# Three changes of order in a four-layer attention and MLP kernel: VectorE's products of blocks 2 and 3, PSUM banks named by hand, and GpSimd's masks behind a normalisation

## The chip, the cores and the metric

One core of a Trainium2 chip runs the whole kernel. Its engines are TensorE (PE in the profile; PEld is its weight load), VectorE (DVE), ScalarE (ACT), GpSimd (POOL) and SyncE (SP, which here only issues DMAs). The metric is device time in microseconds of one execution. The kernel before was run three times: 746.05, 749.81 and 750.95 us, median 749.81 us.

## The reference

Input `x` has 2048 tokens (S) of 576 features (D), in bfloat16. Four residual layers follow one another: A, B, A, B, the two A's with the same weights and the two B's too.

```python
def _A_ref(x, wqkv, wo):          # 32 heads of 18 features
    q, k, v = ...                  # x @ wqkv, split in heads
    phi = lambda t: jnp.where(t > 0, t + 1, jnp.exp(t)) + 1e-6
    pq, pk = phi(q), phi(k)
    kv = einsum("bhsd,bhse->bhde", pk, v);  z = einsum("bhsd->bhd", pk)
    num = einsum("bhqd,bhde->bhqe", pq, kv)
    den = einsum("bhqd,bhd->bhq", pq, z)[..., None] + 1e-6
    return heads_joined(num / den) @ wo
def _B_ref(x, w1, b1, w2, b2):     # F = 4608
    h = gelu(layernorm(x) @ w1 + b1)
    return h @ w2 + b2
x = x + _A_ref(layernorm(x));  x = x + _B_ref(layernorm(x));  # and both again
```

A is linear attention: the keys of all 2048 tokens have to be summed before any output exists, and each output is divided by a denominator of its own head and token.

## The kernel before

**Layout.** The tokens are cut into 16 tiles of 128 (index `t`) and into 4 blocks of 512 (index `c`, four tiles each). `x_sb` holds all of x; `yT` holds the normalised x with the features on the partitions, which is what the projections read; `units` is a set of 37 slots of 128x512 that hold the queries `pq[(g, c)]` of five groups of heads (`g`) and later the MLP's hidden values.

**Order.** All engines' instructions are recorded in the program's order: the wrapper classes (L53) and `pe` (L229) chain each engine's instructions as they are written. What an engine does next is thus fixed by the source, and a wait of one instruction holds all that stand behind it on that engine.

**PSUM.** The eight banks have names. `accA` and `accB` are pairs of banks and are given out in turn by `pair()`; `one0` to `one3` are single banks, given out in turn by `one()`, which counts `one_turn["n"]` up and takes it modulo 3 or 4. A tag that is given by hand leaves the counter alone. A matmul that opens a bank waits until its last reader is done.

**Layer A, first part (the first layer only: `placed` is False).** A loop over the 16 tiles. In iteration `t` TensorE transposes the normalised tile `t+2` (`tp`, L468), computes the keys of tile `t+1` (`k_ps`, two halves), and adds tile `t` into `rk_ps` and `side_ps`; in five of the iterations (1, 2, 3, 8 and 14) it also projects a query tile (`q_ps`). VectorE in the same iteration (`mid_tile0`, `k_finish`) normalises tile `t+3` (`y_ring`), takes the statistics of tile `t+4` (`ln_st`, `ln_mv`), and then finishes the keys of tile `t+1` (a `phi_e`, and two `pk` instructions, the last of which frees a key bank). GpSimd turns the variance into 1/sqrt (`ln_u`, `ln_rstd`), which the next iteration's normalisation waits for. Ten batches of masks (`mask_batches`: memsets and `affine_select`s for `maskz`, `zsel`, `head_sel`, `quad_mask`, and `head_bc` in four batches called `spread`) are made by GpSimd in iterations 2 to 11, one in each, released by the `pk` that ends `k_finish`.

**Layer A, second part (both A layers).** The sums become a matrix `kvwo` of each group of heads, and the queries that are left are projected. `wo_stage` computes the output of block 0's four tiles, and VectorE adds each to `x_sb` (`residual`); the four tiles are normalised for the MLP at once (the list `first`: two by ScalarE, two by VectorE) and transposed through `tp` banks, while TensorE goes on with `q_next` (a query tile each) and ends with `q_batch`, which does the last four query tiles together in four banks. ScalarE reads each query bank twice (Exp, Relu); in `q_batch` ScalarE and VectorE read one each.

**Layer A, third part.** The denominators of blocks 1 to 3 are computed (`den_stage`), inverted (`reciprocal`), written to DRAM and read back spread over the heads (`spread`, into `yT`). `scales(c)` multiplies block `c`'s five query tiles with them: five VectorE instructions (four of 128x512, one of 128x256), `units<-yT,units`, each of which waits for its own DMAs. `outputs(c)` is two `wo_pair`s: 36 matmuls each on row tiles into one pair of banks and two single ones, and then three VectorE additions into `x_sb`, which free the banks. `groups(n)` puts groups of the next MLP's first product between (`m1_group`: four hidden blocks in a pair, `hp_ps`, and two singles, `h_ps`, evicted by ScalarE with gelu). The third part's order is in the last lines of `layer_A`. TensorE's part of it: two groups, the denominators, four groups, outputs 1, a group, outputs 2, a group, outputs 3.

**Layer B.** For each block the rest of its nine groups, and then `m2_ps` = hidden values times w2, added to `x_sb`.

Of the kernel before, what the change touches and what calls it, by code (L numbers as in the profile page):

```python
# [35 lines left out]
def build(tc, A_x, A_wqkv, A_wo, B_w1, B_b1, B_w2, B_b2, out, n_layers=4):  # L36
    nc = tc.nc
    with ExitStack() as ctx:
# [22 lines left out]
        SYNC = mybir.DependencyInfo(mybir.DependencyClass.Sync, mybir.DependencyReason.DATA)  # L61
        vec, act = InOrder(nc.vector, "VectorE"), InOrder(nc.scalar, "ScalarE")
# [16 lines left out]
        one_turn = dict(n=0, banks=4)  # L79
# [122 lines left out]
        units = const.tile([P, NF + 1, CB], BF16, name="units")  # L202
# [28 lines left out]
        def row_tiles(ops_of, dst, relay, after):  # L231


            order = [(hi, op) for step in zip([op for n in (0, 1, 2, 3) for op in ops_of(n, 0)],
                                              [op for n in (2, 3, 0, 1) for op in ops_of(n, 1)]) for hi, op in enumerate(step)]
            first, final, total = {}, {}, [0] * 4
            for i, (hi, (n, _, _)) in enumerate(order):
                first.setdefault((hi, n), i)
                final[(hi, n)] = i
                total[n] += 1  # L240
            relay_at = {max(final[(0, a)], final[(1, b)]): (a, b) for a, b in ((0, 2), (1, 3))}
            starts = {first[(1, 0)]: 0, first[(0, 2)]: 2, first[(1, 1)]: 1, first[(0, 3)]: 3}
            relay_of, seen = {}, [0] * 4
            for i, (hi, (n, wt, mv)) in enumerate(order):
                ins = mm(dst[n], wt, mv, seen[n] == 0, seen[n] == total[n] - 1)
                seen[n] += 1
                if i in starts:
                    tc.add_manual_dep(ins.ins, relay_of[starts[i]], SYNC, reason="row tiles take turns on a PSUM bank")
                if i in relay_at:
                    passed = relay()  # L250
                    tc.add_manual_dep(passed.ins, ins.ins.name, SYNC, reason="row tiles take turns on a PSUM bank")
                    for m in relay_at[i]:
                        relay_of[m] = passed.ins.name
                after(n, [a == b for a, b in zip(seen, total)], relay_at.get(i))
# [247 lines left out]
        def by_token(ap, placed):  # L502

            return ap.rearrange("p (t b q) -> p b t q", t=4, b=4) if placed else ap

        def as_read(ap, placed):
            return ap.rearrange("p (b t q) -> p b t q", b=4, t=4) if placed else ap
# [21 lines left out]
        def warm_table(func):  # L529
            act.activation(out=act_dummy[:, 0:1], in_=neg_half[:, 0:1], func=func)  # L530
# [21 lines left out]
        def layer_A(li, next_kind, begin, before_tile, before_keys, mid_tile, rows_ahead, after_tile, q_tiles, placed, mlp):  # L552
# [21 lines left out]
            def k_sum(t, half):  # L574
                cols = slice(half * HALF, (half + 1) * HALF)
                vec.tensor_scalar(out=es[t][:, cols], in0=es[t][:, cols], scalar1=1.0, scalar2=1e-6, op0=ALU.min, op1=ALU.add)
                return vec.scalar_tensor_tensor(out=pks[t][:, cols], in0=kps.pop((t, half))[:, 0:HALF], scalar=0.0,
                                                in1=es[t][:, cols], op0=ALU.max, op1=ALU.add)
# [82 lines left out]
            def q_batch(es, tags):  # L661
                c = q_left[0][1]
                del q_left[0:4]
                dst = [(one_of if tag in ("accA", "accB") else one)("q_ps", tag) for tag in tags]

                def ops_of(g, hi):
                    rows, cols = HALVES[hi], slice(c * CA, (c + 1) * CA)
                    ops = [(g, wq_sb[rows, k, g, :], yT[rows, k, cols]) for k in range(KD - 1)]
                    if g % 2 == hi:
                        ops.append((g, q_tail[:, g // 2, :] if hi else wq_sb[rows, KD - 1, g, :], yT[rows, KD - 1, cols]))  # L670
                    return ops

                evicted = set()

                def after(n, done, turn):
                    if not done[n] or n in evicted:
                        return
                    evicted.add(n)
                    to = pq[(n, c)] = units[:, slot_of[(n, c)], :]
                    e = es[n]  # L680
                    act.activation(out=by_token(e, placed), in_=as_read(dst[n][:], placed), func=ACT.Exp)
                    vec.tensor_scalar(out=by_token(to, placed), in0=as_read(dst[n][:], placed), scalar1=0.0, scalar2=None, op0=ALU.max)
                    q_late.append(lambda: q_sum(to, e))

                row_tiles(ops_of, [q[:] for q in dst], relay_by_pool, after)
# [122 lines left out]
            def q_sum(dst, e):  # L808
                vec.tensor_scalar(out=e, in0=e, scalar1=1.0, scalar2=1e-6, op0=ALU.min, op1=ALU.add)
                vec.tensor_tensor(out=dst, in0=dst, in1=e, op=ALU.add)  # L810
# [10 lines left out]
            def finish(n):  # L821
                for _ in range(n):
                    q_late.pop(0)()

            def q_next(late=False, tag=None, between=None, evict=None):
                q_proj(*q_left.pop(0), late, tag, between, evict)
# [21 lines left out]
            for t in range(0 if placed else NT):  # L848
# [15 lines left out]
                if t == 1:  # L864
                    done = k_sum(2, 1)
                mid_tile(t)
                rows_ahead(t)
                if 1 < t < NT - 1:
                    done = k_finish(t + 1)
# [175 lines left out]
            first = [Norm(t, "B", "act" if i < 2 else "dve", "act" if i < 2 else "dve") for i, t in enumerate((0, 2, 1, 3))]  # L1045
# [50 lines left out]
            for t in range(TPC):  # L1096
                wo_stage((0, 2, 1, 3)[t])
                if t == 1:
                    first[0].norm()
                first[t].stats()  # L1100
                first[t].rstd()
                if t == 2:
                    first[1].norm()
                if t == (0 if placed else 1):
                    q_next(True)
                if t == 3:
                    first[0].transposed()
            other = [("accA", "accB")[(pair_turn["n"] + i) % 2] for i in (1, 0)]
            q_next(True)
            first[2].norm()  # L1110
            q_next(True, other[0])
            first[1].transposed()
            q_next(True, other[1])
            if placed:
                q_next(True)
            first[3].norm()
            finish(1)
            first[2].transposed()
            first[3].transposed((other[0],))
            finish(3)  # L1120
            q_batch([units[:, i, :] for i in range(13, 17)], ("one2", "one1", "one3", other[1]))
            warm_table(ACT.Gelu_apprx_tanh)
            assert not q_left

# [1 line left out]
            def scales(c):  # L1126
                for g in range(G):
                    scale_stage(g, c)

            def groups(n, late=()):  # L1130

                for i in range(n):
                    last = bool(late) and i == n - 1
                    mlp.m1_group(0, mlp.done, relay_by_pool, elsewhere)
                    if last:
                        for step in late:
                            step()
                    mlp.flush()

            def outputs(c):  # L1140
                for j in range(2):
                    wo_pair(c, j)
# [10 lines left out]
            spread(3)  # L1153
            scales(1)
            groups(4)
            scales(2)
            outputs(1)
            groups(1)
            scales(3)
            outputs(2)  # L1160
            groups(1)
            outputs(3)

# [115 lines left out]
        norms = [Norm(t, "A", "act" if t == 3 else "dve", "halves" if t < 3 else "act", t < 3) for t in range(NT)]  # L1279
# [54 lines left out]
        batches = mask_batches()  # L1334
# [4 lines left out]
        def before_keys0(t, ys):  # L1339
            if 0 < t < NT - 2:  # L1340
                norms[t + 2].transposed()
                ys[t + 2] = norms[t + 2].y

        def mid_tile0(t):
            if t == 0:
                return
            ahead = [norms[t + 4].stats, norms[t + 4].rstd] if t + 4 < NT else []
            if t + 3 < NT:

                ahead.insert(2 if t == 2 else 0, norms[t + 3].norm)  # L1350
            for step in ahead:
                step()

# [3 lines left out]
        def after_tile0(t, done):  # L1357
            for _ in range(2 if t == 1 else 1):
                if late_pieces:
                    late_pieces.pop(0)()  # L1360
            if 2 <= t < 2 + len(batches):
                first = batches[t - 2]()
                tc.add_manual_dep(first.ins, done.ins.name, SYNC, reason="beside VectorE's statistics")
            if t == NT - 1:
                transpose_b1()

# [61 lines left out]
```

## Time and profile before

| | |
|---|---|
| median of three runs | 749.81 us |
| the profiled execution's own time | 747.97 us |
| its span in the profile | 746.2 us |
| granted TensorE clock, mean | 0.999 |
| VectorE busy | 272.0 us (36%) |
| ScalarE busy | 297.3 us (40%) |
| GpSimd busy | 132.2 us (18%) |
| first A layer, tiles' loop | about 11 to 55 us |
| first A layer, block 0's outputs to the last query | about 66 to 81 us |
| first A layer, blocks 1 to 3 | about 89 to 129 us |
| second A layer, blocks 1 to 3 | about 454 to 493 us |

The span runs from the first to the last instruction of the program; the execution's own time has some 1.8 us more around it. The stages' times are read from the timeline by the names of the tiles. In the timeline a row merges like instructions: start, duration of the whole row, engine, line, operation, tiles, shapes, count, and in brackets how long the engine was idle before it and what ended that idle time. The chain of work that ended last is given as start, length and what ran.

### The profile page before, as it was taken

What the parts mean: (1) busy time and instruction counts of PE and PEld (TensorE: products, weight loads), DVE (VectorE), ACT (ScalarE), POOL (GpSimd) and SP (SyncE); (2) the same over time, 40 slices, a digit from 0 to 9 for tenths busy, and PEclk for the clock granted to TensorE, in tenths of its full rate; (3) what the DMA queues carried; (4) which work ended last, traced back from release to release, by engine and by line L of the source; (5) the groups of instructions that cost most, each with busy time, mean ns of one, the idle gap of its engine ahead of it and who ended that gap; (6) DMA issues with size and microseconds to landing.
All of it is one profiled execution on the core that took longest, in us unless ns stands there. A gap on an engine that the chain in (4) does not pass through costs nothing.

```text
span 746.2 us, 16672 instructions
## 1 busy us (share of the span) xinstructions
PE 738.9 (99%) x6951; PEld 475.9 (64%) x6951; DVE 272.0 (36%) x674; ACT 297.3 (40%) x642; POOL 132.2 (18%) x403
## 2 busy tenths in 40 slices
PE   8999999999999999999999999999999999999998
PEld 4666556774477457646777665777646754774476
DVE  8878725533124402400366685542401140100000
ACT  5766652106700750274035666320273047106700
POOL 4641000322122201200213120021200120010010
PEclk9999999999999999999999999999999999999999
DMA  7946120022011202110023101202000200020000
GB/s 201 241 152 209 64 85 19 8 53 44 2 22 39 44 2 32 44 30 2 17 72 92 33 1 36 69 1 52 18 1 9 52 10 1 16 45 10 1 9 25
DMA packets 61297, 34.74 MB, mean 47 GB/s; under 512 B 37126, under 2 KB 61222, under 8 KB 61222
## 3 DMA queue, kind: packets, MB, share of 16 engines
q1 hardware_dynamic: 60470, 33.45, 17.8%
q8 instruction: 54, 0.88, 0.5%
q10 hardware_dynamic: 752, 0.23, 0.1%
q14 instruction: 21, 0.17, 0.1%
HBM read 21.70 MB, written 4.93 MB: 36 GB/s over the span
## 4 chain that ended last, share of the span: by engine, by line
PE 94%; DVE 3%; ACT 1%; DMA 1%; POOL 1%; issue 0%; SPq 0%; DVEq 0%; POOLq 0%
PE m_ps L229 38%; PE hp_ps L229 20%; PE h_ps L229 17%; PE k_ps L229 4%; PE q_ps L229 4%; PE wo_ps L229 4%; PE rk_ps L229 3%; DVE ln_st L53 1%; DVE y_ring L53 1%; PE side_ps L229 1%; ACT units L53 0%; PE tp L468 0%; DVE units L53 0%; DMA yT<-rden_rows 0%; POOL ln_rstd L53 0%
## 5 line engine op out<-in xcount | busy, mean ns | idle before, releaser
L229 PEld LDWEIGHTS <-units 128*128 128x128 bf16 (+1 forms) x2926 | 266.1, 97 | 67.9 <-issue 3.6
L229 PE MATMUL m_ps<-w_sb,units 128*128 128x288 bf16 (+2 forms) x2288 | 283.0, 286 | 0.0
L229 PEld LDWEIGHTS <-w_sb 64*128 64x128 bf16 x2304 | 127.7, 94 | 133.6 <-issue 4.0
L229 PE MATMUL h_ps<-yT,w_sb 64*128 64x512 bf16 x1152 | 174.0, 376 | 0.0
L229 PE MATMUL hp_ps<-yT,w_sb 64*128 64x512 bf16 x1152 | 151.4, 376 | 1.7 <-DVE x_sb L53 1.7
L53 DVE TENSOR_TENSOR x_sb<-m_ps,xo 128x576 bf16<-128x576 f32 (+3 forms) x34 | 24.4, 721 | 323.7 <-PE m_ps L229 323.7
L53 ACT ACTIVATE units<-hp_ps,b1T 128x512 bf16<-128x512 f32 x144 | 91.2, 684 | 88.5 <-PE hp_ps L229 88.5
L53 ACT COPY relay_sb<-relay_sb 128x1 f32<-128x1 f32 x112 | 21.4, 191 | 235.6 <-PE hp_ps L229 224.7
L53 ACT ACTIVATE units<-h_ps,b1T 128x512 bf16<-128x512 f32 x142 | 95.2, 687 | 0.0
L53 POOL TENSOR_TENSOR xo<-x_sb,b_bc 128x576 f32<-128x576 bf16 x32 | 40.8, 1274 | 302.8 <-DVE x_sb L53 291.3
L229 PE MATMUL k_ps<-wkv_sb,yT 64*128 64x288 bf16 (+3 forms) x432 | 61.4, 299 | 0.4 <-ACT yT L53 0.2
L229 PE MATMUL hp_ps<-yT,w_tail 64*128 64x512 bf16 x144 | 54.1, 376 | 0.0
L229 PE MATMUL h_ps<-yT,w_tail 64*128 64x512 bf16 x144 | 54.1, 376 | 0.0
L53 DVE BATCH_NORM_STATS2 ln_st<-x_sb 128x6 f32<-128x288 bf16 x128 | 51.2, 440 | 1.1 <-DMA x_sb<-in_A_x_dram 0.8
L53 DVE STREAM_TRANSPOSE shared<-y_ring 128x640 bf16<-128x640 bf16 x40 | 32.9, 826 | 41.2 <-DMA yT<-shared 39.1
L53 ACT ACTIVATE phi_e<-k_ps 128x288 bf16<-128x288 f32 x64 | 26.3, 413 | 54.0 <-PE k_ps L229 50.2
L53 DVE TENSOR_SCALAR y_ring<-x_sb,ln_mv,ln_rstd 128x576 bf16<-128x576 bf16 (+2 forms) x60 | 33.3, 557 | 24.5 <-POOL ln_rstd L53 24.0
L229 PEld LDWEIGHTS <-yT 64*128 64x128 bf16 (+1 forms) x448 | 36.4, 95 | 8.9 <-ACT yT L53 0.5
L229 PE MATMUL q_ps<-yT,wq_sb 64*128 64x512 bf16 (+2 forms) x282 | 41.9, 349 | 0.0
L53 POOL MEMSET pool_relay<- 128x1 f32 x152 | 16.7, 110 | 127.9 <-PE hp_ps L229 45.4
L229 PE MATMUL wo_ps<-shared,units 64*128 64x288 bf16 (+1 forms) x480 | 38.0, 283 | 0.0
L229 PEld LDWEIGHTS <-w_tail 64*128 64x128 bf16 x288 | 27.1, 94 | 16.9
(110 smaller groups left out, 501.4 us busy)
## 6 DMA issues: line engine op xcount, KB each, us to landing
yT<-shared SPq DMA_DIRECT2D x160, 40.0 KB
w_sb<-in_B_w_dram SPq DMA_DIRECT2D x12, 432.0 KB
w_sb<-in_B_w_dram SPq DMA_DIRECT2D x9, 512.0 KB
yT<-rden_rows SPq DMA_DIRECT2D x24, 126.0 KB
y_rows<-y_ring SPq DMA_DIRECT2D x16, 144.0 KB
units<-y_rows SPq DMA_DIRECT2D x16, 144.0 KB
x_sb<-in_A_x_dram SPq DMA_DIRECT2D x15, 144.0 KB
out_dram<-x_sb SPq DMA_DIRECT2D x15, 144.0 KB
```

What stands on the lines that cost most here:

```text
L53: inst = issue(*args, **kw)
L229: return pe(nc.tensor.matmul(out_, lhsT=lhsT, rhs=rhs, start=start, stop=stop, **kw))
```

## The change

Three parts, all of them a matter of order or place. No instruction is added or taken out on any engine, and TensorE's, ScalarE's, GpSimd's and SyncE's orders are as before; VectorE's order changes in the third part of both A layers alone.

1. **Products behind outputs.** The third part's order, seen by VectorE, was products 1, products 2, additions 1, products 3, additions 2, additions 3. It becomes products 1, additions 1, products 2, additions 2, products 3, additions 3.
2. **Banks by hand.** In the first A layer's second part the query tiles and transposes take banks that are named, and `one_turn["n"]` is set to 3 behind `q_batch`. In the order of TensorE, the banks of the twelve opened there were one1, one2, one3, accA, one0, accB, one1, accA for query, transpose, query, query, transpose, query, transpose, transpose, and one2, one1, one3, accB for the batch's four; they become one0, one2, accA, one1, one3, one0, one2, accA, and accB, one3, one1, one2. From there to the end of the next MLP the single banks are the same turn shifted by two.
3. **Masks behind a normalisation.** Batch `i` was issued at the end of iteration `i+2` behind the last `pk` of `k_finish`; it is issued in iteration `i+3` behind that iteration's normalisation. On GpSimd it stands in the same place between two tiles' `ln_rstd`.

```diff
@@ second part
                 if t == (0 if placed else 1):
-                    q_next(True)
+                    q_next(True, None if placed else "one0")
                 if t == 3:
-                    first[0].transposed()
+                    first[0].transposed((None if placed else "one2",))
             other = [("accA", "accB")[(pair_turn["n"] + i) % 2] for i in (1, 0)]
-            q_next(True)
+            q_next(True, None if placed else other[0])
             first[2].norm()
-            q_next(True, other[0])
-            first[1].transposed()
-            q_next(True, other[1])
+            q_next(True, other[0] if placed else "one1")
+            first[1].transposed((None if placed else "one3",))
+            q_next(True, other[1] if placed else "one0")
             if placed:
                 q_next(True)
             first[3].norm()
             finish(1)
-            first[2].transposed()
+            first[2].transposed((None if placed else "one2",))
             first[3].transposed((other[0],))
             finish(3)
-            q_batch([units[:, i, :] for i in range(13, 17)], ("one2", "one1", "one3", other[1]))
+            q_batch([units[:, i, :] for i in range(13, 17)],
+                    ("one2", "one1", "one3", other[1]) if placed else (other[1], "one3", "one1", "one2"))
+            if not placed:
+                one_turn["n"] = 3
@@ third part
             scales(1)
             groups(4)
+            outputs(1)
             scales(2)
-            outputs(1)
             groups(1)
+            outputs(2)
             scales(3)
-            outputs(2)
             groups(1)
             outputs(3)
@@ masks
+        def norm_and_masks(t):
+            norms[t + 3].norm()
+            if 2 < t < 3 + len(batches):
+                first = batches[t - 3]()
+                tc.add_manual_dep(first.ins, vec.last, SYNC, reason="beside VectorE's statistics")
+
         def mid_tile0(t):
...
-                ahead.insert(2 if t == 2 else 0, norms[t + 3].norm)
+                ahead.insert(2 if t == 2 else 0, lambda: norm_and_masks(t))
...
-            if 2 <= t < 2 + len(batches):
-                first = batches[t - 2]()
-                tc.add_manual_dep(first.ins, done.ins.name, SYNC, reason="beside VectorE's statistics")
```

## The prediction

> **What bounds the kernel now.** I read the page's busy shares first, then its chain that ended last, and then the chain and the timeline of the three stretches that the change touches.
>
> ```profile
> PE 738.9 (99%) x6951; PEld 475.9 (64%) x6951; DVE 272.0 (36%) x674; ACT 297.3 (40%) x642; POOL 132.2 (18%) x403
> ...
> PE 94%; DVE 3%; ACT 1%; DMA 1%; POOL 1%; issue 0%; SPq 0%; DVEq 0%; POOLq 0%
> ```
>
> TensorE is the bound: 94% of the chain is its own work, which the change does not touch. The change can only win stretches in which TensorE stood still, so I took the distance from each matmul's start to the next one's and looked where it is longer than the columns need. Behind the start (up to 12 us) only these are over 0.2 us: 0.25 at 43.3 and 0.25 at 46.2 (masks), 0.41 at 76.0 (banks), 0.21 at 81.7, 1.85 at 110.2 (products) and 0.20 at 388.8. All that the change could remove is thus some 3 us of 746.
>
> **Part 1, products behind outputs.** The timeline of the first A layer:
>
> ```profile
> 105.67 0.90 PE L229 MATMUL wo_ps<-shared,units 64*128 64x288 bf16 x10
> ...
> 107.70 1.43 DVE L53 TENSOR_TENSOR units<-yT,units 128x512 bf16<-128x512 bf16 x4 [4.88 <-DMA yT<-rden_rows]
> ...
> 111.14 0.29 DVE L53 TENSOR_TENSOR units<-yT,units 128x256 bf16<-128x256 bf16 x1 [2.00 <-DMA yT<-rden_rows]
> 111.34 2.87 DVE L53 TENSOR_TENSOR x_sb<-wo_ps,x_sb 128x576 bf16<-128x576 f32 x6
> 112.14 1.04 PE L229 MATMUL hp_ps<-yT,w_sb 64*128 64x512 bf16 x8 [1.69 <-DVE x_sb L53]
> ```
>
> Outputs 1 start at 105.67. Their six additions stand on VectorE behind block 2's products, whose fifth waits until 111.14 for a DMA. The next group (`hp_ps`) needs the bank of the first addition and starts at 112.14, 6.47 us after the outputs did. In the second A layer that DMA was earlier, and the same stretch has no stall:
>
> ```profile
> 471.16 0.90 PE L229 MATMUL wo_ps<-shared,units 64*128 64x288 bf16 x10
> ...
> 475.80 1.04 PE L229 MATMUL hp_ps<-yT,w_sb 64*128 64x512 bf16 x8
> ...
> 479.68 0.77 PE L229 MATMUL wo_ps<-shared,units 64*128 64x288 bf16 x9
> ```
>
> There it is 475.80 - 471.16 = 4.64 us. So the first layer loses 6.47 - 4.64 = 1.83 us, the second nothing.
>
> With the new order the additions wait for the outputs' matmuls alone, as those of outputs 2 do already: in the first layer these start at 116.03, their additions at 118.45 and 120.66, 2.42 and 4.63 us later, three in 1.49 us, and the next group starts at 120.44 without a stall. So the 1.83 us go. What is late next? Block 2's products now start behind the last addition. From a start W of outputs 1: the last three additions at W + 4.86 (4.63, and 0.23 more, as this stretch takes 4.64 where that of outputs 2 takes 4.41), done at W + 6.35; five products, 1.34 to the fifth's start and 0.29 for it, done at about W + 8.0; outputs 2 start at W + 4.64 + 3.88 (475.80 to 479.68) = W + 8.52. Half a microsecond is left. For block 3: additions done at 4.63 + 1.49 = 6.12, products at 7.8, outputs 3 at 4.41 + 3.88 = 8.29: again 0.5. The DMAs are no limit there: block 2's last data came 5.5 us after W (111.14 - 105.67), block 3's were used at 116.41, 10.7 after W, where the new order asks for them at about W + 14. Five waits move onto TensorE's weight loads of the first five operands; all are over by then, so I count them as nothing. **Value: -1.83 us in the first layer, 0 in the second.** Ends: -2.0, and, if the margin of 0.5 fails by as much in all four places, +2.0 - 1.83 = +0.2.
>
> **Part 2, banks.** Rows around the last transposes:
>
> ```profile
> 74.37 2.06 ACT L53 ACTIVATE units<-q_ps 128x512 bf16<-128x512 f32 x4
> ...
> 75.95 0.18 DVE L53 COPY y_ring<-y_ring 128x64 bf16<-128x64 bf16 x1
> ...
> 76.48 0.44 PE L468 MATMUL tp<-ident,y_ring 128*128 128x128 bf16 x5 [0.25 <-ACT units L53]
> ```
>
> ScalarE reads two query tiles here, the first until 75.46 and the second until 76.43. The last transpose takes `accA`, before the change the second's bank; its data are ready at 75.95 + 0.18 = 76.13. After it, `accA` is the first's bank, free at 75.46, so the transposes start at about 76.17, 0.31 earlier. The batch behind them then opens `one1`, the second's bank, with its second matmul, which can start at 76.43 + 0.05 = 76.48 instead of 76.87: 0.39 gained over the two. Inside the batch one start lies 0.12 us late at 78.06, where `accB` waits for the next query tile, read until 78.00; after the change the batch's fourth bank is `one2`, last copied out by VectorE at 77.26, just before it is wanted (76.46 + 4 steps of 0.24 = 77.4). The stall of 0.21 us at 81.74 stays: the hidden block that starts there takes, before and after, the bank of the batch's third tile, evicted at 82.11 by VectorE behind ScalarE, and that work follows TensorE forward. ScalarE itself runs without a gap from 70.7 to 78.0, from the first normalisation's 1/sqrt on, so it does not follow these 0.4 us; the banks it frees are those I used. The closest new wait is the query tile that now takes `accA`: free at 71.66 (third block-0 addition), wanted at 72.04. **Value: -0.5 us.** Ends: -0.7 (the third stall too) and +0.3 (that margin used up and nothing gained).
>
> **Part 3, masks.** The chain in the tiles' loop:
>
> ```profile
> 40.18 0.58 POOL ln_rstd L53
> 40.76 0.03 issue
> 40.78 0.94 DVE y_ring L53
> 41.73 0.73 DVE ln_st L53 x2
> ...
> 43.09 0.58 POOL ln_rstd L53
> 43.66 0.03 issue
> 43.69 0.94 DVE y_ring L53
> ```
>
> A normalisation starts when the 1/sqrt ends, and so does the mask batch; the two collide. Alone it takes 0.42 us (14.41), beside the `head_bc` batch 0.94, beside `quad_mask`'s select and `head_bc`'s memset 1.35 (34.14). The tile then takes 2.91 us (40.78 to 43.69) on this chain, where TensorE needs 2.66 (transposes at 25.45, 28.11 and 30.77). From the transposes at 30.77 to those at 48.46 there are six tiles and one query tile: 17.69 us, against 6 x 2.66 + 1.08 = 17.04. **0.65 us are lost in all.**
>
> After the change the batch starts when the normalisation ends. Its neighbours are then the statistics, which take 0.44 and 0.44 us beside a 0.64 us select (32.05) and without one (36.0) alike. But GpSimd's next 1/sqrt stands behind the batch: 0.42 + 0.06 (a wait's delay, 18.56 to 18.62) + 1.40 (batch at 40.75) + 0.3 + 0.6 (`ln_u`, `ln_rstd`) = 2.78 us a tile, still 0.12 over TensorE's 2.66, for the three `spread` batches that a 1/sqrt follows: 0.36, less what the earlier batches, now shorter, leave in hand. I take 0.2 us of stall left: **-0.45 us.** Ends: -0.65, and +0.5, if `phi_e` is held as the normalisation was.
>
> That is where a rule speaks against the change. The rows: beside a select the statistics keep their 0.44 us and the normalisation loses 0.5. The Trainium skill (SBUF — State Buffer, Who interferes with whom) says that VectorE in a two-port mode and GpSimd share a port pair, held for a whole instruction by whichever issued first, and that an instruction with one SBUF input outside these modes doesn't contend; the rows fit. By that rule the batch's tail now blocks the `phi_e`.
>
> **The sum:** -1.83 - 0.5 - 0.45 = -2.8 us. Nothing behind gives it back: from the last query to 129 us TensorE had no other stall over 0.1 us, and the DMAs of the denominators start from TensorE's own work and move with it. Span 746.2 to 743.4, the execution's own time 747.97 to 745.2. The median of the runs shown is 1.84 above the profiled one and the lowest 1.92 below; the mean of all four is 748.7, less 2.8 is **745.9 us**, which I forecast. No change that a measurement of this kernel can tell (1%, 7.5 us) comes out of it.
>
> **Rivals.**
> - *The products' stall belongs to this one execution.* The second layer shows the same code without it, as its DMA came in time; where that holds in the first layer too, part 1 gives nothing, and the sum is -0.95: own time 747.0, by the mean 747.8. For it: the gap hangs on one DMA's landing; against: w2's pieces are in the queues ahead of it only in the first layer. 0.18.
> - *The masks' stall moves to `phi_e`.* By the rows the batch runs from 0.48 to 1.88 after the normalisation's start and `phi_e` is due at 1.30; held to the end of the select that runs then, 0.25 to 0.4 us, it ends `k_finish` at 2.27 + 0.4 = 2.67, TensorE's own pace. So part 3 gives about nothing: sum -2.3, own time 745.6, by the mean 746.4. 0.20.
> - *The products come too late (slower).* VectorE has 8.5 - 4.9 = 3.6 us between the last output's matmul and the next output's first; it needs 3.1. From 1.2 times as long it stalls TensorE in all four places; at 1.5 times, 4.7 us, by 1.1 each, 4.4 less 2.8 is +1.6: own time 749.6, by the mean 750.3. Against: the additions (0.75, 0.45) and products (0.42, 0.29) keep their times in both layers, and GpSimd has only 0.10 us memsets here. 0.05.
> - *The parts hold but the run's spread hides them:* not a case of its own; it widens the range.
>
> The forecast has 0.57. All cases lie within 1% of the median. With the lowest run 1.9 below and the highest 3.0 above the profiled one, the range goes from 745.2 - 1.9 - 1 = 742.3 to 749.6 + 1.4 = 751. Faster by over 1% (below 742.3) 0.04, within 1% 0.93, slower by over 1% (above 757.3) 0.03.
>
> **What would show it.** Part 1: additions some 2.4 us after each outputs' start, `hp_ps` 4.6 us after the first outputs', products of 128x512 then in a row without a DMA wait, no idle of TensorE on VectorE's `x_sb`. Part 2: no wait of `tp` for ScalarE. Part 3: every `y_ring` near 0.42, transposes 2.66 to 2.8 apart to 48 us. Wrong if `wo_ps` of outputs 2 or 3 waits for `units` from VectorE, or if a query or transpose waits longer for its new bank.

## The result, and the profile after

The changed kernel takes **744.88 us** (median of 13 runs, 744.64 to 745.07); the kernel before, beside it, 748.70 us (13 runs, 746.05 to 750.95). The ratio is 0.9951 with a 95% interval of 0.994 to 0.9963: half a per cent faster. That lies within the 1% that the prediction called no change; but the interval leaves out 1, so 13 runs of each do tell the two apart, which the prediction said no measurement of this kernel would. The profiled execution took 745.07 us with a span of 743.4 us and a granted clock of 1.0, against 747.97 and 746.2 before. Two things stand out ahead of any row. The profiled pair differs by 2.9 us, the medians by 3.8. And the runs of the kernel before lie 4.9 us apart, those of the changed one 0.43 us: what was taken out was not a constant.

First the page of the changed kernel, its busy times and the shares of the chain that ended last:

```profile
PE 737.0 (99%) x6942; PEld 479.2 (64%) x6951; DVE 268.8 (36%) x674; ACT 297.3 (40%) x642; POOL 131.7 (18%) x403
...
PE 98%; DVE 1%; DMA 1%; SPq 0%; issue 0%; DVEq 0%
```

VectorE had 3% of the chain, ScalarE and GpSimd 1% each; now TensorE's own work is 98% of it. The last 1% of DMA is the load of the input at the start.

**Part 1.** The third part of the first A layer, from the timelines of VectorE and TensorE of the changed kernel (start, length, then what; the bracket is the idle time ahead and what ended it):

```profile
104.72 0.90 PE L229 MATMUL wo_ps<-shared,units 64*128 64x288 bf16 x10
...
107.33 1.49 DVE L53 TENSOR_TENSOR x_sb<-wo_ps,x_sb 128x576 bf16<-128x576 f32 x3 [5.19 <-PE wo_ps L229]
...
109.30 1.06 PE L229 MATMUL hp_ps<-yT,w_sb 64*128 64x512 bf16 x8
...
109.54 1.49 DVE L53 TENSOR_TENSOR x_sb<-wo_ps,x_sb 128x576 bf16<-128x576 f32 x3 [0.72 <-PE wo_ps L229]
110.94 1.62 DVE L53 TENSOR_TENSOR units<-yT,units 128x512 bf16<-128x512 bf16 x5
...
113.18 0.77 PE L229 MATMUL wo_ps<-shared,units 64*128 64x288 bf16 x9
```

The additions wait for outputs 1 alone, 2.6 us after these start. The next group comes 109.30 - 104.72 = 4.58 us after them, where it was 6.47, and waits for nobody. The five products run in a row without a DMA wait, and outputs 2 follow at 113.18. So 1.89 us went here. The second A layer has the same picture: `hp_ps` 472.87 - 468.33 = 4.54 us behind the outputs, where it was 4.64.

**Part 2.** Around the last transposes of the changed kernel (timeline):

```profile
71.78 2.32 PE L229 MATMUL q_ps<-yT,wq_sb 128*128 128x512 bf16 x10
...
74.11 2.06 ACT L53 ACTIVATE units<-q_ps 128x512 bf16<-128x512 f32 x4
...
75.53 0.73 PE L468 MATMUL tp<-ident,y_ring 128*128 128x128 bf16 x10
...
76.19 2.11 PE L229 MATMUL q_ps<-yT,wq_sb 64*128 64x512 bf16 x17
...
81.20 1.04 PE L229 MATMUL h_ps<-yT,w_sb 64*128 64x512 bf16 x8
```

The ten transposes of two tiles run through in 0.73 us, without the wait for ScalarE, and the batch of queries behind them too. From the query tile ahead of them (71.78) to the first `h_ps` block of the MLP (81.20) there are 9.42 us. The same two rows of the kernel before are 10.12 us apart:

```profile
72.04 2.32 PE L229 MATMUL q_ps<-yT,wq_sb 128*128 128x512 bf16 x10
...
82.16 1.04 PE L229 MATMUL h_ps<-yT,w_sb 64*128 64x512 bf16 x8
```

**Part 3.** The chain in the tiles' loop of the changed kernel, its transposes only:

```profile
31.16 0.28 PE tp L468 x5
...
40.23 0.28 PE tp L468 x5
...
42.89 0.28 PE tp L468 x5
...
45.55 0.28 PE tp L468 x5
...
48.21 0.28 PE tp L468 x5
```

They come 2.66 us apart, TensorE's own pace, and 48.21 - 31.16 = 17.05 us, where it was 17.69 (30.77 to 48.46). The normalisations have left the chain.

Laid beside each other weight load by weight load, the two traces differ as follows. Positive is time that the kernel before lost; the start is the time until TensorE's 61st weight load, ahead of everything that was changed.

| stretch | us |
|---|---|
| start of the program | -0.39 |
| tiles' loop (masks) | 0.64 |
| last transposes and queries, to the MLP (banks) | 0.72 |
| first A layer, behind outputs 1 (products) | 1.87 |
| second A layer, the same place | 0.07 |
| all else | under 0.02 |
| sum | 2.9 |

### The profile page after: what moved, and what is told of

It reads as the page before. It is cut to its first block, busy times and chain, and to the rows that moved or that the text cites. A ratio compares the mean times of both kernels' runs of the same rounds, so it can differ in the third digit from the quotient of the medians.

```text
span 743.4 us, 16663 instructions
## 1 busy us (share of the span) xinstructions
PE 737.0 (99%) x6942; PEld 479.2 (64%) x6951; DVE 268.8 (36%) x674; ACT 297.3 (40%) x642; POOL 131.7 (18%) x403
## 4 chain that ended last, share of the span: by engine, by line
PE 98%; DVE 1%; DMA 1%; SPq 0%; issue 0%; DVEq 0%
PE m_ps L229 38%; PE hp_ps L229 20%; PE h_ps L229 17%; PE k_ps L229 5%; PE q_ps L229 5%; PE wo_ps L229 5%; PE rk_ps L229 4%; PE tp L468 1%; PE side_ps L229 1%; DMA x_sb<-in_A_x_dram 1%; SPq L53 0%; PE den_ps L229 0%; PE kvwo_ps L229 0%; PE kv_ps L229 0%; PE rden_ps L229 0%; DVE pk L53 0%
## 5 line engine op out<-in xcount | busy, mean ns | idle before, releaser
L229 PEld LDWEIGHTS <-w_sb 64*128 64x128 bf16 x2304 | 129.2, 94 | 129.8 <-issue 2.1
L229 PE MATMUL q_ps<-yT,wq_sb 64*128 64x512 bf16 (+2 forms) x273 | 40.4, 347 | 0.4
L53 DVE TENSOR_SCALAR y_ring<-x_sb,ln_mv,ln_rstd 128x576 bf16<-128x576 bf16 (+2 forms) x60 | 30.3, 506 | 24.5 <-POOL ln_rstd L53 24.3
```

Source lines behind the costliest of these rows:

```text
L53: inst = issue(*args, **kw)
L229: return pe(nc.tensor.matmul(out_, lhsT=lhsT, rhs=rhs, start=start, stop=stop, **kw))
```

## The experiments

Twelve experiments ran, in three groups, each on a chip of its own and with its own runs of the kernel before (e1 to e4, e5 to e8, e9 to e12). Each trace was laid beside that of the changed kernel in the same way; this gives, for each profiled execution, what it lost in each of the four places (e7 and e8, whose losses are of another kind, stand in their own part). The table is used all through this section.

| profiled execution | own time | start, us | masks | banks | products, layer 1 | layer 2 |
|---|---|---|---|---|---|---|
| before | 747.97 | 11.76 | 0.64 | 0.72 | 1.87 | 0.07 |
| before, again (e11) | 747.95 | 11.77 | 0 | 0.72 | 2.1 | 0.47 |
| part 1 (e1) | 746.71 | 12.47 | 0.63 | 0.72 | 0 | 0 |
| part 2 (e2) | 747.37 | 11.92 | 0 | 0 | 1.97 | 0.54 |
| part 3 (e3) | 747.83 | 11.94 | 0 | 0.72 | 1.78 | 0.5 |
| part 3, again (e12) | 748.17 | 12.08 | 0 | 0.72 | 1.72 | 0.73 |
| parts 2 and 3 (e4) | 745.37 | 12.10 | 0 | 0 | 0.3 | 0.06 |
| parts 1 and 2 (e5) | 744.60 | 11.66 | 0 | 0 | 0 | 0 |
| block 1's data (e6) | 746.55 | 12.25 | 0.64 | 0.72 | 0 | 0 |
| before, late transfers (e9) | 749.00 | 11.73 | 0 | 0.72 | 1.57 | 2.0 |
| after, late transfers (e10) | 744.73 | 11.73 | 0 | 0 | 0 | 0 |
| after | 745.07 | 12.15 | 0 | 0 | 0 | 0 |

The own times follow from it: 744.65 us, and the start's excess over 11.73, and the row's losses. For e11 that is 744.65 + 0.04 + 0.72 + 2.1 + 0.47 = 747.98, measured 747.95; for e12 744.65 + 0.35 + 0.72 + 1.72 + 0.73 = 748.17, measured 748.17. In these twelve executions nothing else moves by more than 0.02 us.

### One part at a time

e1 to e4 are the kernel before with part 1, with part 2, with part 3, and with parts 2 and 3, each part as the change's diff has it. e1 for instance:

```
             groups(4)
+            outputs(1)
             scales(2)
-            outputs(1)
             groups(1)
+            outputs(2)
             scales(3)
-            outputs(2)
```

> The kernel before with part 1 alone (products behind outputs). Before it 13 runs of the kernel before lay between 746.05 and 750.95 us (median 748.7), and 13 of the changed one between 744.64 and 745.07 (median 744.88): the profiled executions differ by 2.9 us, the medians by 3.8, and the spread shrinks from 4.9 to 0.4 us. Theory: the spread and the rest of the gain are one thing, the wait of block 2's fifth product for its DMA in the first A layer, 1.83 us in the profiled run and longer or shorter in others. Then part 1 alone takes the spread away: 746.2 us (744.9 and the 1.3 us of the other two parts), all runs within 1 us, no wait of hp_ps for x_sb. Rival A: the spread comes from elsewhere, the first loads or the tiles' loop; then part 1 alone gives 1.9 us, 746.8 us, and the runs still spread over 4 us.

> The kernel before with part 2 alone (banks by hand). Theory: 0.7 us less than before, about 748.0 us, and the spread of before stays (4 to 5 us), as the products still wait for the DMA. In the profile the stretch from the two query tiles at 72.0 us to the second kind of hidden block at 82.2 us shortens from 10.1 to 9.4 us. Rival A (the spread comes from the stretch ahead of the products): the spread shrinks here or with part 3. Rival B (the parts' gains overlap, as the DMA's landing is what sets outputs 1's end, so what is won ahead of it is waited for again): 0, 748.7 us.

> The kernel before with part 3 alone (masks behind a normalisation). Theory: 0.65 us less, about 748.05 us, the spread of before stays; normalisations of 0.42 us each and transposes 2.66 us apart in the tiles' loop. Rival A: the spread shrinks. Rival B: the gain is waited for again at block 2's products, 748.7 us.

> The changed kernel without part 1 (parts 2 and 3 alone). Theory: 1.3 us less than before, about 747.4 us, runs spread over 4 to 5 us, the lowest near 744.9, where the DMA came in time. Rival A: the spread is small without part 1 too. Rival B (gains ahead of the DMA are waited for again): 748.7 us.

Measured, beside 35 runs of the kernel before with a median of 748.04 us (745.79 to 750.2):

| kernel | median (runs; lowest to highest) | ratio, 95% interval |
|---|---|---|
| e1, part 1 | 745.68 (11; 745.45 to 746.71) | 0.9975 (0.9965 to 0.9984) |
| e2, part 2 | 746.18 (12; 745.38 to 749.17) | 0.9986 (0.9976 to 0.9997) |
| e3, part 3 | 746.56 (12; 745.91 to 747.83) | 0.9985 (0.9975 to 0.9996) |
| e4, parts 2 and 3 | 746.00 (11; 745.37 to 746.99) | 0.9979 (0.9971 to 0.9988) |

Part 1 is the largest, and nine of its eleven runs lie within 0.52 us. The forecasts (746.2, 748.0, 748.05 and 747.4 us) were all too high, by 0.5, 1.8, 1.5 and 1.4 us. The spread was forecast to stay at 4 to 5 us without part 1. It did in e2 (3.8 us); but e3's runs lie 1.9 us apart and e4's 1.6, hardly more than e1's 1.3, as the rival "the spread is small without part 1 too" had it. So these four don't show that part 1 alone takes the spread away; that rests on e6, e9 and e10 below.

The table of losses says more than the medians. In e4, which keeps the old order of the products, the first layer lost only 0.3 us. Its timeline of VectorE:

```profile
106.35 1.43 DVE L53 TENSOR_TENSOR units<-yT,units 128x512 bf16<-128x512 bf16 x4 [4.66 <-DMA yT<-rden_rows]
...
108.56 0.29 DVE L53 TENSOR_TENSOR units<-yT,units 128x256 bf16<-128x256 bf16 x1 [0.78 <-DMA yT<-rden_rows]
```

The fifth product waited 0.78 us for its DMA, where it waited 2.00 in the trace before; the order of work is the same. And in e2 and e3 the second layer, which I had taken for free of the stall, lost 0.5 us. So the products' stall has a different size in each execution, in both layers, and one trace shows one draw of it.

The traces' DMA packets show what the size goes with. Block 2's last four transfers make 128 packets of 512 bytes. In the first layer of before, e2, e3, e11 and e12, 127 of them end by 3.3 to 3.7 us after outputs 1 start, and one ends at 4.1 to 4.4 us, 0.03 to 0.06 us behind a single packet of 16,384 bytes of the kind `instruction` that lasted about 1 us; the fifth product starts 1.26 to 1.34 us behind that packet. In e4 the instruction packet begins at 3.64 us, when the last data packet has already ended at 3.22, and the product starts at 3.89. In the second layer a packet of 8,192 bytes stands there: in e2, e3, e11 and e12 the last data packet ends 0.02 to 0.03 us behind one and 0.47 to 0.73 us are lost, while in before and e4 none ends close ahead of it and 0.06 to 0.07 us are lost. So the long waits are those in which such an `instruction` packet ran just ahead of the last data packet. This is read from the traces; no run moved these packets.

What the medians of e2, e3 and e4 gained beyond the traced worth of their parts, 0.7 to 1.1 us each with the masks counted at 0.64, is not explained: shorter waits for that DMA would do it, but only the profiled executions have a trace, and those of e1 and e3 were the longest of their 11 and 12 runs. The longest runs have another mark. Nine runs of the three groups had a mean granted clock of 0.998 or less, and they are the longest of their kernel in their group (749.16 to 750.2 among the 35, 749.17 in e2, 749.62 and 749.88 among the 26 beside e5 to e8, 750.77 to 752.52 in e9); the changed kernel's 13 runs all had 1.0. None of the nine was traced, so whether a long wait lowered the clock or the clock lengthened the run stays open.

### Is it the DMA, or the order of the work?

Three kernels change what the products wait for and leave the order as it is. e6 is the kernel before, except that block 2's products read the denominators of block 1, whose data are long there (block 2 is multiplied by the wrong denominators, and all else is kept):

```
-    in0=spare(c)[...]
+    in0=spare(1 if c == 2 else c)[...]
```

e9 is the kernel before, and e10 the changed one, each with four small transfers more on SyncE's queue, behind the first of the three batches of denominators in both layers. They make block 2's transfers issue some 1.36 us later and touch rows that nobody reads then:

```
         spread(1)
+        for i in range(4):
+            sp.dma_start(out=rden_rows[0][8*i:8*i+8, 0:P], in_=ident[0:8, :])
```

> The kernel before, with block 2's products multiplied by block 1's denominators, which landed long ago (so the output of block 2 is another; all instructions are there, only the wait for block 2's own DMAs is gone). Theory: that wait alone is what part 1 takes off the path. Then this is as fast as part 1 alone, 745.7 us, its runs spread by about 1 us, and hp_ps does not wait for x_sb, although VectorE's order is the old one. Rival (the order is what counts, the additions are late behind the products anyhow): a stall stays, and the time lies between 746.5 and 748.

> The kernel before with four more small DMAs on SyncE (8 rows of 256 bytes each, to rows of DRAM that nobody reads) behind block 1's spread, in both A layers, so that block 2's and block 3's data land 1.6 to 3 us later. Theory: in the kernel before block 2's landing sets the first addition, so the delay is paid in full in the first layer and less some tenths in the second: 3 to 6 us slower than before. Rival (the additions wait for something else): under 1 us.

> The changed kernel with the same four DMAs. Theory: block 2's products are not wanted before 7 us or more after the outputs' start, and landed at 5.5 us at the latest, so 1.6 to 3 us more fit but for a few tenths: 744.9 to 746 us, a spread under 1 us. Rival (the wait was only moved to the next outputs): slower by as much as e9_late_before.

Measured: e6 745.77 us (12 runs, 745.32 to 746.72) against 746.92 (26 runs), ratio 0.9979 (0.997 to 0.9988), and no wait on `x_sb` in either layer. That is e1's time, 745.68, without e1's order: the wait for block 2's own transfers is all of part 1.

e9 749.56 us (10 runs, 749.0 to 752.52) against 746.58 (17 runs), ratio 1.0044 (1.0031 to 1.0057); e10 744.78 us (8 runs, 744.64 to 745.32), ratio 0.9973 (0.9962 to 0.9984). From the timelines of e9, TensorE in both layers and VectorE in the second:

```profile
111.20 1.04 PE L229 MATMUL hp_ps<-yT,w_sb 64*128 64x512 bf16 x8 [1.41 <-DVE x_sb L53]
...
473.47 1.43 DVE L53 TENSOR_TENSOR units<-yT,units 128x512 bf16<-128x512 bf16 x4 [6.78 <-DMA yT<-rden_rows]
...
475.78 0.29 DVE L53 TENSOR_TENSOR units<-yT,units 128x256 bf16<-128x256 bf16 x1 [0.88 <-DMA yT<-rden_rows]
...
476.80 1.04 PE L229 MATMUL hp_ps<-yT,w_sb 64*128 64x512 bf16 x8 [1.84 <-DVE x_sb L53]
```

Now the second layer stalls as the first: DMA to product, product to addition, addition to bank, bank to `hp_ps`. The median rose by 3.0 us, about two layers of 1.36 and the lower end of the 3 to 6 us that were forecast. The trace doesn't bear out the forecast that the first layer pays in full: it lost 1.57 us there, no more than most did without the delay. Its data came 1.4 us after the last issue, where it took 2.6 to 3.2 us in five of the other six; this time the instruction packet had ended (4.26 us after outputs 1 started) before the last data packet (4.62). The changed kernel, with the same late transfers, has no bracket on its products at all:

```profile
110.52 1.62 DVE L53 TENSOR_TENSOR units<-yT,units 128x512 bf16<-128x512 bf16 x5
```

A delay that costs the old order 3 us costs the new one nothing. That is what part 1 buys. It fits that the worth of the change differs from one group of runs to the next: the changed kernel, or its near copies e5 and e10, took 744.77 to 744.88 us in the three groups that hold one of them, while the kernel before had medians of 748.7, 746.9 and 746.6 there, and 748.0 in the group of e1 to e4. As each group had a chip of its own, the chip may have a part in that; no run tells the two apart.

### How much margin has the new order?

The slower rival was that block 2's products come too late. e7 and e8 are the changed kernel with three or six statistics of no use between an output's additions and the next block's products, in all four places (the code is shortened):

```
         outputs(1)
+        for _ in range(3):            # e8: 6
+            vec.bn_stats(out=st[:, 0, :], in_=x_sb[:, 0, 0:HALF])
         scales(2)
```

> The changed kernel with three more VectorE instructions (statistics of a half tile that nobody reads, 0.37 us each in a row, 1.1 us) between the additions and the products of blocks 2 and 3, in both A layers: four places. In the changed kernel's trace the fifth product ends 0.6 us ahead of the next outputs' start (112.56 and 113.18), but outputs 2 need the products one after the other: the fifth is wanted some 0.5 us after the first. Theory A (each weight load waits for its own product): 1.1 us more still fit, loss under 0.5 us in all. Theory B (as the prediction counted, a margin of 0.5 to 0.6 us to the fifth product): 0.5 us in each of four places, +2.0 us.

> As with three, but six more VectorE instructions (2.2 us) in each of the four places. Theory A: 2.2 - 1.1 = 1.1 us in each place, +4.4 us, 749.3 us. Theory B: 1.6 in each, +6.5 us, 751.4 us. If the margin is not the products' but hidden by something else: no loss.

Measured: e7 744.83 us (5 runs, 744.69 to 745.09), ratio 0.9965 (0.995 to 0.998); e8 749.05 us (8 runs, 748.93 to 749.46), ratio 1.0023 (1.0013 to 1.0034). The timeline of e7, where the products start 1.09 us later than in the changed kernel:

```profile
110.94 1.17 DVE L53 BATCH_NORM_STATS2 ln_st<-x_sb 128x6 f32<-128x288 bf16 x3
...
112.03 1.61 DVE L53 TENSOR_TENSOR units<-yT,units 128x512 bf16<-128x512 bf16 x5
...
113.18 0.81 PE L229 MATMUL wo_ps<-shared,units 64*128 64x288 bf16 x9
```

and of e8, whose outputs 1 started at 104.44, 0.28 earlier than there:

```profile
110.66 2.25 DVE L53 BATCH_NORM_STATS2 ln_st<-x_sb 128x6 f32<-128x288 bf16 x6
...
112.82 1.61 DVE L53 TENSOR_TENSOR units<-yT,units 128x512 bf16<-128x512 bf16 x5
...
113.29 1.50 PE L229 MATMUL wo_ps<-shared,units 64*128 64x288 bf16 x9 [0.18 <-DVE units L53]
```

In e7 the outputs start while the products still run (113.18 against 112.03 + 1.61 = 113.64), and lose 0.03 us: each weight load waits for its own product, not for the fifth. In e8 the products stand 112.82 - 104.44 = 8.38 us behind outputs 1, where the changed kernel has 110.94 - 104.72 = 6.22: 2.16 later. The nine matmuls stretch from 0.77 to 1.50 us, and by the weight loads each of the four places loses 1.04 to 1.11 us. 2.16 - 1.11 = 1.05 us is the margin, and e7's 1.09 - 0.03 = 1.06 says the same. The rival's mechanism is real, but the point from which it decides lies twice as far off as I had put it: by my 0.5 us e8 would have lost 1.66 us a place.

### What are the masks worth?

The trace of e2 made me ask: it has the old masks, and lost nothing in the tiles' loop. e5 is the changed kernel with the masks put back as they were (parts 1 and 2); e11 is the kernel before, once more, and e12 part 3 alone, once more.

> The changed kernel without part 3 (parts 1 and 2 alone). In the profiled executions so far, the tiles' loop loses 0.64 us in that of the kernel before and of part 1 alone, and nothing in that of part 2 alone, though all three have the masks as before: there the normalisation issued 0.16 us ahead of the batch (40.53 and 40.69) and kept its 0.42 us, where otherwise the batch issued 0.04 us ahead of it. Theory: a race between the two that some executions lose and others win, so that part 3 is worth 0.64 us in some and nothing in others: runs in two heaps, one at the changed kernel's 744.9 us and one at 745.5, and a median of 744.9 to 745.5. Rival (the 0.64 us are lost in nearly all executions, the profile of part 2 alone is the exception): one heap at 745.5.

> The kernel before once more, for another profile of its two stalls. In the six profiles of kernels that keep the old order of products the first layer's stall was 1.83, 1.96, 1.76 and 0.28 us and the second layer's 0, 0.46, 0.43 and 0, the tiles' loop lost 0.64 or nothing. Theory: other values in the same ranges, and the execution's own time is 745.4 (no stall, banks as before) and the sum of the three, give or take the start's 0.0 to 0.7 us. Rival: a time that the three stalls don't explain.

> Part 3 alone once more: its median of 746.56 us lay 1.5 us under the kernel before's in the same comparison, where the masks can give no more than 0.64. Theory: the rest is block 2's landing, shorter in these executions by chance; this profile then shows a first-layer stall anywhere between 0.3 and 2.0 us and the time that belongs to it. Rival: the masks themselves shorten something else, which the profile would show outside the tiles' loop and the products.

e5 took 744.77 us (6 runs, 744.60 to 745.33), ratio 0.9962 (0.995 to 0.9974): as fast as the changed kernel's 744.88. e11's profiled execution took 747.95 us and e12's 748.17, and the losses in the table give both times. e11's 2.1 us in the first layer lie above the four stalls listed for it, e12's 1.72 inside its range. The timeline of the kernel before, in the first trace, with the mask batch on GpSimd and the normalisation on VectorE:

```profile
40.75 1.40 POOL L53 TENSOR_SCALAR_AFFINE_SELECT head_bc<-head_bc 128x504 bf16<-128x504 bf16 x4
40.78 0.94 DVE L53 TENSOR_SCALAR y_ring<-x_sb,ln_mv,ln_rstd 128x576 bf16<-128x576 bf16 x1
```

and of e11, the same kernel in another execution (its two normalisations around 34 and 40, and the mask work beside them):

```profile
34.15 0.78 DVE L53 TENSOR_SCALAR y_ring<-x_sb,ln_mv,ln_rstd 128x576 bf16<-128x576 bf16 x1
34.71 0.79 POOL L53 MEMSET head_bc<- 128x640 bf16 x1
...
40.39 0.42 DVE L53 TENSOR_SCALAR y_ring<-x_sb,ln_mv,ln_rstd 128x576 bf16<-128x576 bf16 x1
40.55 1.45 POOL L53 TENSOR_SCALAR_AFFINE_SELECT head_bc<-head_bc 128x504 bf16<-128x504 bf16 x4 [0.36 <-DVE pk L53]
```

In the first trace the batch starts 0.03 us ahead of the normalisation, which then takes 0.94 us. In e11 it starts 0.16 us behind and the normalisation takes 0.42; the transposes stay 2.66 us apart and the loop loses nothing (30.78 to 47.84 in its chain, 17.06 us). Either order holds itself up. Where the normalisations run in time, the batch has to wait for the tile's last `pk` (the 0.36 in the bracket) and comes second. Where they are late, `pk` is long done when the 1/sqrt ends, both are released by that at once, the batch comes first, and the next normalisation is late again. They part at 34 us: in e11 the normalisation gets in between `quad_mask`'s select and `head_bc`'s memset (0.78 us, and the memset takes 0.79), in the first trace behind both (1.35 us). Of seven traces with the old masks three lose the 0.63 to 0.64 us (before, e1, e6) and four don't (e2, e5, e9, e11). What sends an execution into one order or the other is not settled. e6's twelve runs lie in two heaps, about 745.4 and 746.1, and two of e1's eleven 1 us above the rest; that fits a loss of 0.64 us taken by some, but the start varies as much, and those runs have no trace. The sum under the table gives a bound, as an estimate: with the earliest start seen (11.66) a run that takes the loss needs at least 745.2 us in e5 and 745.9 us in e1 and e6, which keep the old banks. Five of e5's six runs, eight of e1's eleven and six of e6's twelve lie below that, so most runs escaped it. Of e5's two expectations neither came out as written: there is one heap, at 744.6 to 745.1 us with one run at 745.33, and it lies at the changed kernel's time, not at 745.5. The race itself is in the traces.

So part 3 takes away a loss that some executions have. In the median of the finished kernel it is worth nothing that six runs can tell, and no kernel of the twelve experiments is clearly faster than the changed one.

## Why the prediction was right, and where it was not

The time was forecast at 745.9 us and came out at 744.88, inside the range. That range, 742.3 to 751 us, held the forecast and every rival, so lying inside it does not tell them apart. The 748.7 us from which the forecast started were the median of before; all of the 1.0 us that it missed by is in the gain, 3.8 instead of 2.8. The span was forecast at 743.4 us and was 743.4, which is partly luck: the parts took out 3.3 us rather than 2.8, and this execution began 0.39 us later than the one before.

- **What bounds the kernel.** Right. Reading the distances between matmuls found all the places where there was something to win but for the 0.07 us of the second A layer: nothing outside the four stretches differs by over 0.02 us. "Some 3 us" was the size in one execution.
- **Part 1, the mechanism.** Right as worked out: additions off the DMA, `hp_ps` 4.58 us behind the outputs (forecast 4.64), products in a row, five new waits of TensorE's weight loads at no cost. Its value in the profiled pair is 1.94 us, forecast 1.83. e6 shows that the wait for block 2's transfers is the whole of it.
- **Part 1, "-1.83 us in the first layer, 0 in the second".** This is the step that failed. It takes one execution's wait for the kernel's. In the six traces that have the old order and nothing added (before, e2, e3, e4, e11, e12) the first layer lost 0.3 to 2.1 us and the second 0.06 to 0.73. With values from the middle of these six, 1.8 and 0.5 us, the change would be worth 3.0 us, or 3.7 with the masks' loss, where the medians differ by 3.8; the rest is not shown. The first rival, that "the products' stall belongs to this one execution", was right that it varies, and wrong in seeing the variation only downward: in these six the second layer was a lucky one and the first was an ordinary one. What I held against it, that w2's pieces stand in the queues only in the first layer, is not what made the difference: around the last data packet the traces show an instruction packet, in either layer.
- **Part 1, the margin: "half a microsecond is left".** Mis-sized; it is 1.05 us. I counted to the end of the fifth product, but the outputs' first matmuls need the first product alone (e7, e8).
- **Part 2, "-0.5 us".** Mis-sized; 0.72 us, just beyond the lower end of -0.7 that I gave for the case that "the third stall too" goes. The step that failed is "the stall of 0.21 us at 81.74 stays": 0.18 of it went. I had let the eviction move with TensorE; it moved by more. VectorE's eviction ends 0.97 us earlier than before (82.11 to 81.14), the last matmul ahead of the waiting block starts 0.79 us earlier (81.74 to 80.95), and behind it the next one still starts when the eviction is done (81.20). Why the two moved apart is not shown.
- **Part 3, "-0.45 us".** In the profiled pair 0.64, all of the loss. "The two collide" is the step that failed: they collide so that it costs time in some executions alone. The 0.2 us that I left standing did not stay either. GpSimd's batch does make the normalisations come 2.84 and 2.97 us apart (40.76, 43.60, 46.57), but the transposes did not follow. What TensorE had waited for was the last `pk` (done at 43.57, its weight load at 43.63); with the normalisations back at 0.42 us it is done 0.11 us ahead of the weight load (46.17 and 46.28).
- **The masks' rival, that the stall moves to `phi_e`.** Fell. `phi_e` took 0.35 and 0.37 us instead of 0.31 beside `quad_mask`'s select and `head_bc`'s memset (33.41, 36.07): 0.04 to 0.06, off the chain, where the rival needed 0.25 to 0.4. Beside `head_bc`'s selects it kept its 0.31. The Trainium skill (SBUF — State Buffer, Who interferes with whom) has the port pair held by whichever instruction issued first; the race of the masks agrees with that, normalisation 0.94 us when the select was 0.03 ahead, 0.42 when it was 0.16 behind.
- **The products too late.** Did not happen; in e8, 1.1 us beyond the margin that e7 and e8 show, it does, and costs that 1.1 us in each place.

## What to carry to other kernels

An instruction that waits for a DMA, in an in-order queue ahead of the work that frees the next stage's banks, has no constant cost: each execution draws another. Put it behind that work where its data are wanted late enough, and test the margin by adding idle work there. When a stall in a profile hangs on a DMA's landing or on which of two engines issues first, read the spread of the times, or a second profile of the same kernel, before pricing it: here one trace gave the parts 2.8 us, and the medians of three groups of runs put the worth of the changed kernel or its near copies at 1.8 (e10), 2.2 (e5) and 3.8 us. In e7 and e8 a weight load that needs one product waited for that product, so here the margin has to be counted from the first product to its own consumer, and not to the last product.

## What the hardware showed that I had not expected

- **Landing times.** SyncE issues block 2's nine transfers one after the other, 0.3 to 0.8 us each, and in the trace before the last issue ends 2.46 us after outputs 1 start in the first layer and 2.06 in the second. From the end of the last issue to the first use of its data by the product that waited for it went 1.4 us (e4), 1.6 (second layer of the trace before), 3.0 (first layer) and 3.1 (e2): the same nine transfers, in the same program or nearly so. The two long ones are those whose last data packet ended just behind an `instruction` packet of 16,384 bytes.
- **A stall that some executions have.** The normalisation and the mask batch settle, in one execution of one program, into an order that lasts for the rest of the loop, and whether one normalisation at 34 us takes 0.78 or 1.35 us goes with which.
- **The start.** The 61st weight load, the first anchor after the input's load, came at 11.66 to 12.47 us in fourteen profiled executions, all of them the same code up to there. For differences below 1 us two spans can't be compared until this is taken off.
